# A planned attention kernel: the second half of each output sum gets another priority, and three figures of the planner change

## The chip, the cores and the metric

The kernel runs on one core of a Trainium2 chip. The metric is the device time of one execution in microseconds (us); lower is better. Before the change the median of 11 runs is 850.99 us (849.99 to 853.66).

## What is computed

One input `x` of 2048 tokens by 512 goes through two attention blocks with 32 heads of 16, and a gate mixes the two results.

```
x = A_x                                            # [1, 2048, 512] bf16
g = sigmoid((x * gate_w).sum(-1, keepdims=True))
# A: full attention, H=32, Dh=16
scores = einsum("bhqd,bhkd->bhqk", q, k) * Dh**-0.5
a = (softmax(scores) @ v, heads joined) @ A_wo
# B: each token looks at 8 earlier tokens, 2 apart (W, dil = 8, 2)
idx = pos[:, None] - (arange(8) * 2)[None, :]      # masked where idx < 0
b = (softmax(q . k[idx] * Dh**-0.5) @ v[idx], heads joined) @ B_wo
return g * a + (1 - g) * b
```

The gate's factors are folded into the normalisation of the two blocks, so that one output tile of 128 tokens is the sum of eight 128x128x512 matmuls: four with `A_wo`, four with `B_wo`.

## The kernel before

**Tiling.** The scores of block A are made in units: 128 keys by 512 queries of one head. Four heads form a group; 8 groups times 4 chunks of 512 queries make 32 periods (line 506) of 64 units each, 2048 units in all. A score matmul uses 32 rows of TensorE, so up to four heads run side by side. The product of probabilities and values ("PV") uses 17 columns per head, and again four heads side by side. Projections, output sums and transposes use the whole array. TensorE thus changes between three tiling modes: row tiles (scores), column tiles (PV), whole array (the rest).

**The exponential.** ScalarE takes most units. Two rings in PSUM take turns: ring A holds three units, ring B two (`act_stream`, line 972). TensorE fills a ring (`ring<-qt,kt_all`), ScalarE computes one `pT<-ring` over it (128x1536 or 128x1024), then the ring may be filled again. I call the fill of ring A a three-unit fill, that of B a two-unit fill, and the TensorE work that stands between one fill and the next a *slot*; it is named after the fill that opens it. The PV matmuls of five units usually stand together in the slot behind a two-unit fill.

**Units off ScalarE.** Some units are computed instead by VectorE (four passes, `ta<-w`, twice `ta<-ta,w`, `pd<-ta,w`, line 1093) or GpSimd (line 1128). Their scores go to one of two PSUM banks called `w` (line 450). A unit rides along with a fill (`rider`, line 1063) or goes alone (`solo`, line 1043). A *doubled* fill (line 1011) writes the same scores twice, which gives TensorE work at the end of a period, while its accumulator is closed; in other gaps `fill_pass` (line 847) adds matmuls with a zero weight (`acc<-ident,z`).

**Jobs.** Projections for both blocks, transposes and output sums need a `w` bank too. A 512-column job of four matmuls is the commonest. `final_job` (line 1301) makes one output tile: it yields its eight matmuls in two pieces of four (line 1322), the first (`w<-awo,oT`) with priority `30 + tt`, the second (`w<-bwo,obt`) with priority `GO`, 1.9; then VectorE copies the bank out (`osb<-w`, line 1380) and SyncE's queue stores it. Twelve tiles (the first three chunks) have four plus four matmuls; in the last chunk two tiles have seven in such pieces, and two are made by `direct_job` (line 1345) at the end.

**What sets the order.** The program is written out once, by a planner in Python (`class Plan`, line 52), which runs while the kernel is built. Every job is a generator that asks for an engine with a priority, a planned duration and a function that emits the instructions. `run` (line 222) keeps a planned clock for each engine and takes, for the engine that can go first, the ready request of the lowest priority number. The order in which it takes them is the order of the instructions on each engine; on the chip the engines follow it, and semaphores guard the data. What matters for the change:

- Fills have priority 0, PV from ScalarE's units a little over 1, `GO` pieces 1.9, jobs 2 and more.
- `fits` (line 216) lets a TensorE request of priority 2 or more start only if its planned end is not past `limit` (line 185), the planned time at which ScalarE runs out of queued work, less `refill`, 0.52; after 4 us of waiting it yields slowly. A request below 2 is never held by it.
- A TensorE piece of n passes is planned as `n * MM + SW`, with `MM` 0.2135 and `SW` 0.11 (lines 468, 469), the latter for the change of tiling mode; line 284 takes the same 0.11 off when it books how much the array streamed.
- `JW`, 0.8 (line 190), is how much planned VectorE work must be queued before a job that needs a `w` bank may start (`room_for_job`, line 200; it may anyway after 3 us), and above which a rider makes way for a waiting job (line 1074).

All instructions are emitted through one wrapper, so the profile gives all of them line 347; they are told apart by their tiles.

Of the kernel before, what the change touches and what calls it, by code (L numbers as in the profile page):

```python
# [51 lines left out]
class Plan:  # L52
# [13 lines left out]
    held = {"job": 0}  # L66
    streamed = deque()
    cap_job = 2
    refill = 0.52
    patience = 6.0  # L70

    def resource(self, name, n):
# [114 lines left out]

    passes = 0
    calm = False
    JW = 0.8  # L190
    JP = 3.0
    HUNG = 0.0
    ASL = 1.2
# [6 lines left out]
    def room_for_job(self, x, st):  # L200
        return not self.calm or st - x[7] > self.JP or self.dve_work(st) >= self.JW

# [19 lines left out]
    def run(self):  # L222
        while True:
            best = None
            for e, lst in self.ready.items():
                rs = []
                for x in lst:
                    g_ = self.gate(x[6])
                    if g_ is not None:
                        rs.append(max(x[2], g_))  # L230
                if rs:
                    st = max(self.free[e], min(rs))
                    if best is None or st < best[0]:
                        best = (st, 1, e)
            for r, lst in self.reqs.items():
                if lst and self.slots[r]:
                    st = max(min(x[0] for x in self.slots[r]), min(x[2] for x in lst))
                    if best is None or st <= best[0]:
                        best = (st, 0, r)
            if best is None:  # L240
                return
            st, kind, nm = best
            self.now = st
            if kind == 0:
                lst = self.reqs[nm]
                x = min(y for y in lst if y[2] <= st + 1e-9)
                lst.remove(x)
                s = min(y for y in self.slots[nm] if y[0] <= st + 1e-9)
                self.slots[nm].remove(s)
                self.advance(x[3], st, s[1])  # L250
            else:
                lst = self.ready[nm]
                ok = [y for y in lst if y[2] <= st + 1e-9 and self.gate(y[6]) is not None
                      and self.gate(y[6]) <= st + 1e-9]
                x = min(ok, key=lambda y: (y[0], y[1]))
                if nm == "pe" and 1 <= x[0] < 1.5 and st - x[2] < self.DEFER:
                    jobs = [y for y in lst if y[0] >= 2 and y[4] > 0.5 and y[7] <= st
                            and self.gate(y[6]) is not None and self.gate(y[6]) <= st + 1e-9]
                    y = min(jobs, key=lambda y: (y[0], y[1])) if jobs else None
                    if (y is not None and st + y[4] <= self.limit(st)  # L260
                            and (y[6] != "w" or self.room_for_job(y, st))):
                        x = y
                if nm == "pe" and self.feed_dve(st):
                    continue
                if nm == "pe" and x[6] == "w" and not self.room_for_job(x, st):
                    x[2] = max(x[2], st + 0.1)
                    continue
                if nm == "pe" and not self.fits(x, st):
                    for y in ok:
                        y[2] = max(y[2], st + 0.1)  # L270
                    continue
                lst.remove(x)
                if nm == "pe":
                    self.idle_fill(st, 1 + (x[6] is not None))
                if x[6] is not None:
                    slot = self.take(x[6], st)
                    self.held["job"] += x[6] == "w"
                    more = x[5](slot)
                else:
                    more = x[5]()  # L280
                if isinstance(more, float):
                    x[4] += more
                if nm == "pe":
                    self.stream(st, x[4] - 0.11 - self.thin)
                    self.thin = 0.0
                if CFG_DEBUG:
                    LOG.append((st, x[4], nm, getattr(x[3], '__name__', '?'), x[0]))
                self.free[nm] = st + x[4]
                self.advance(x[3], st + x[4] + self.LAT[nm], None)
# [3 lines left out]
def kernel(  # L293
# [62 lines left out]
    def mm(out_, lhsT, rhs, start, stop, **kw):  # L356
        return PE.matmul(out_, lhsT=lhsT, rhs=rhs, start=start, stop=stop, **kw)
# [108 lines left out]
    P.resource("py", 1)  # L466
    P.resource("pp", 2)
    MM = 0.2135
    SW = 0.11
    VP = 0.60  # L470
    GO = 1.9
    UR = 0.7
# [94 lines left out]
    def k_job(i, sc, rel, prio):  # L567
# [6 lines left out]
        def pe(s):  # L574
            w.open(s, [128, QW])
            for c in range(DC):
                mm(w.t[:], wkp[:, c, i].rearrange("p j d -> p (j d)"), xT[:, c, sc * QW:(sc + 1) * QW],
                   c == 0, c == DC - 1)
        yield ("pe", prio, 4 * MM + SW, pe, w.kind)
        k_left[0] -= 1  # L580
# [27 lines left out]
    def kpk_job(b, sc, rel, prio):  # L608
# [5 lines left out]
        def pe(s):  # L614
            w.open(s, [128, QW])
            for c in range(DC):
                mm(w.t[:], wkr[:, c, 128 * (b + 1):128 * (b + 2)], xT[:, c, sc * QW:(sc + 1) * QW],
                   c == 0, c == DC - 1)
        yield ("pe", prio, 4 * MM + SW, pe, "w")
        k_left[0] -= 1  # L620
# [48 lines left out]
    def qpk_job(c_, b, rel, prio):  # L669
# [6 lines left out]
        def pe(s):  # L676
            w.open(s, [128, QW])
            for c in range(DC):
                mm(w.t[:], wqr[:, c, 128 * (b + 1):128 * (b + 2)], xT[:, c, c_ * QW:(c_ + 1) * QW],
                   c == 0, c == DC - 1)  # L680
        yield ("pe", prio, 4 * MM + SW, pe, "w")

# [35 lines left out]
    def v_job(h0, h1, tb, TB, rel, prio):  # L718
# [7 lines left out]
        def pe(t0, t1):  # L726
            def f(s=None):
                if t0 == 0:
                    w.open(s, [128, TB, n])
                for tt in range(t0, t1):  # L730
                    for c in range(DC):
                        mm(w.t[:, tt, :], xT[:, c, (tb + tt) * 128:(tb + tt + 1) * 128],
                           wv[:, c, h0 * DH:h1 * DH], c == 0, c == DC - 1)
                P.thin = (t1 - t0) * (one - 4 * n / 2400.0)
            return f
        step = TB if TB < 8 else TB // 2
        one = 4 * max(0.0555, n / 2400.0)
        for t0 in range(0, TB, step):
            yield ("pe", GO if t0 else prio, one * step + SW, pe(t0, t0 + step)) + (("w",) if t0 == 0 else ())
        yield ("dve", prio, VP, lambda: V.tensor_copy(out=vp_all[:, tb:tb + TB, h0:h1, 0:DH],  # L740
# [9 lines left out]
    def q_job(p, rel, prio):  # L750
# [9 lines left out]
        def pe(s):  # L760
            w.open(s, [128, QW])
            for c in range(DC):
                mm(w.t[:], wqp[:, c, i].rearrange("p j d -> p (j d)"), xT[:, c, c_ * QW:(c_ + 1) * QW],
                   c == 0, c == DC - 1)
        yield ("pe", prio, 4 * MM + SW, pe, "w")
        st = {}

        def absq():
# [4 lines left out]
        yield ("wait", ev_sel[i])  # L773
        yield ("pe", GO, MM + SW, lambda: mm(w.t[:], selk_all[:, i, :], st["a"][:], False, True,
                                               skip_group_check=True))
# [287 lines left out]
    def rider(js, now=None):  # L1063
        now = P.now if now is None else now
        for p in (front[0], front[0] + 1):
# [7 lines left out]
            j = max(opts, key=lambda j_: len(pend[p][j_]))  # L1073
            if flying[0] and (not P.calm or P.dve_work(now) >= P.JW) and any(x[6] and x[0] < 4.0 + 0.3 * min(front[0] + UR, 16.3) for x in P.ready["pe"]):
                return None
# [225 lines left out]
    def final_job(c_, tt, last):  # L1301

        t = c_ * TPC + tt
        ncb = DC - 1 if last else DC
        for cb in range(ncb):
            yield ("wait", ev_ot.setdefault((c_, cb), Event()))
        yield ("wait", ev_obt[NT - 1 if last else t])
        prio = 30 + tt
        w = Bank()
        srcs = [(oT_tiles[c_][:, cb, tt * 128:(tt + 1) * 128], awo[:, cb, :]) for cb in range(ncb)]  # L1310
        srcs += [(obt_tiles[c_][:, cb, tt * 128:(tt + 1) * 128], bwo[:, cb, :]) for cb in range(DC)]

        def pe(a, b):
            def f(s=None):
                if a == 0:
                    w.open(s, [128, D])
                for z in range(a, b):
                    mm(w.t[:], srcs[z][0], srcs[z][1], z == 0, z == len(srcs) - 1)
            return f
        for a in range(0, len(srcs), 4):  # L1320
            b = min(len(srcs), a + 4)
            yield ("pe", GO if a else prio, (b - a) * MM + SW, pe(a, b)) + (("w",) if a == 0 else ())
        final_left[c_] -= 1
        if final_left[c_] == 0:
            yield ("set", ev_final[c_])
        if not last:
            yield from out_steps(t, w, None, prio)
            return

        def part():  # L1330
            if "t" not in fpart:
                fpart["t"] = work.tile([128, TPC, D], FP32, name="fpart", tag="ksh", bufs=2)
            V.tensor_copy(out=fpart["t"][:, tt, :], in_=w.t[:])
        yield ("dve", prio, VP, part)
        yield w.close()
        yield ("wait", ev_last[tt // 2])
        w = Bank("e")

        def tail(s):
            w.open(s, [128, D])  # L1340
            mm(w.t[:], oT_tiles[c_][:, DC - 1, tt * 128:(tt + 1) * 128], awo[:, DC - 1, :], True, True)
        yield ("pe", tt, MM + SW, tail, "e")
        yield from out_steps(t, w, fpart["t"][:, tt, :], tt)
# [353 lines left out]
```

## Time and profile before

| | |
|---|---|
| median of 11 runs | 850.99 us (849.99 to 853.66) |
| the profiled execution | 850.25 us, span 848.4 us |
| granted TensorE clock | 0.999 |
| ScalarE busy | 826.5 us, 97% of the span |
| VectorE busy | 765.8 us, 90% |
| TensorE busy | 756.2 us, 89% (matmuls in flight, not array at its peak) |
| GpSimd busy | 725.5 us, 86% |
| score activations | 717: 359 of 128x1536, 358 of 128x1024 |
| first and last of them start at | 17.84 us and 837.56 us |

The span is the time from the first to the last instruction; the execution has 1.85 us around it. An engine's busy time is the union of its instructions' times. Two neighbouring activations overlap in their records (a 128x1536 one lasts 1620 ns on average, a 128x1024 one 1197 ns, together 2.82 us, while a pair of them comes every 2.23 to 2.29 us), so a pause between them shows as idle time only after the overlap is used up. The distance from start to start is the better measure.

### The profile page before, as it was taken

How to read it: one execution, taken by the hardware profiler on the slowest of the kernel's cores; microseconds unless marked ns; L12 is line 12 of the kernel's file. 1: busy time of each engine (PE TensorE's matmuls, PEld its weight loads, DVE VectorE, ACT ScalarE, POOL GpSimd, SP SyncE). 2: the span in 40 equal slices, each digit the busy share in tenths (PEclk: the TensorE clock that was granted, in tenths of full speed). 3: DMA queues.
4: the chain of work that ended last, by engine and by line, in shares of the span. 5: the costliest groups of instructions: out<-in, count | busy, mean ns of one | idle time of the engine just before them, and what ended most of it. 6: DMA issues, size and time to landing. Idle time of an engine off the chain costs nothing.

```text
span 848.4 us, 15781 instructions
## 1 busy us (share of the span) xinstructions
PE 756.2 (89%) x5864; PEld 266.8 (31%) x5864; DVE 765.8 (90%) x1332; ACT 826.5 (97%) x748; POOL 725.5 (86%) x734
## 2 busy tenths in 40 slices
PE   9999999989998888888998988888898998888887
PEld 4432343333323332223333232333223233222222
DVE  5698889899999899998999899999989899999896
ACT  5999999999999999999999999999999999999996
POOL 2596886999799999899999999999899999997781
PEclk9999999999999999999999999999999999999999
DMA  9002304411444041303122413120313221201000
GB/s 295 6 14 88 100 27 140 153 64 39 129 118 163 27 130 31 112 19 100 39 89 71 129 34 130 58 81 8 106 32 112 87 83 24 63 13 58 14 1 26
DMA packets 72589, 63.84 MB, mean 75 GB/s; under 512 B 20528, under 2 KB 69168, under 8 KB 72512
## 3 DMA queue, kind: packets, MB, share of 16 engines
q1 hardware_dynamic: 71312, 62.57, 24.1%
q8 instruction: 46, 0.75, 0.4%
q10 hardware_dynamic: 1200, 0.26, 0.2%
q14 instruction: 31, 0.25, 0.1%
HBM read 46.14 MB, written 12.62 MB: 69 GB/s over the span
## 4 chain that ended last, share of the span: by engine, by line
ACT 66%; issue 20%; PE 11%; DMA 1%; DVE 1%; SPq 0%; ACTq 0%
ACT pT L347 65%; PE w L347 4%; PE ring L347 3%; PE acc L347 2%; ACT lg L347 1%; DMA xr<-in_A_x_dram 1%; DVE ta L347 0%; PE s L347 0%; SPq L347 0%; PE e L347 0%; DVE pd L347 0%; DVE qpk L347 0%; DVE osb L347 0%; DVE kvs L347 0%; ACT osc L347 0%
## 5 line engine op out<-in xcount | busy, mean ns | idle before, releaser
L347 ACT ACTIVATE pT<-ring 128x1536 bf16<-128x1536 f32 x717 | 816.5, 1409 | 6.7 <-PE ring L347 3.7
L347 PE MATMUL ring<-qt,kt_all 32*128 32x512 bf16 x1841 | 284.9, 380 | 82.6 <-ACT pT L347 70.2
L347 DVE SCALAR_TENSOR_TENSOR ta<-ta,w 128x512 f32<-128x512 f32 x476 | 317.3, 681 | 5.6
L347 POOL TENSOR_TENSOR prod<-prod 128x512 f32<-128x512 f32 (+1 forms) x208 | 240.4, 1166 | 5.5
L347 PE MATMUL acc<-pT,vp_all 128*17 128x512 bf16 x1793 | 221.4, 383 | 1.3 <-DVE accS L347 0.9
L347 PEld LDWEIGHTS <-kt_all 32*128 32x128 bf16 x2096 | 113.0, 91 | 335.8 <-issue 325.7
L347 PE MATMUL acc<-ident,z 128*17 128x512 bf16 (+5 forms) x773 | 197.3, 341 | 1.4 <-POOL ident masks.py:199 1.4
L347 DVE TENSOR_SCALAR ta<-w 128x512 f32<-128x512 uint16 x238 | 162.6, 686 | 36.4 <-PE w L347 34.3
L347 DVE SCALAR_TENSOR_TENSOR pd<-ta,w 128x512 uint16<-128x512 f32 x238 | 160.2, 678 | 2.5
L347 POOL TENSOR_TENSOR prod<-ksh,qb 128x512 f32<-128x512 bf16 x128 | 144.8, 1156 | 2.2
L347 POOL TENSOR_TENSOR prod<-vsh,lg 128x512 f32<-128x512 bf16 x128 | 136.7, 1098 | 2.8 <-DMA vsh<-kv_scr 0.3
L347 PE MATMUL w<-qt,kt_all 32*128 32x512 bf16 x255 | 95.5, 383 | 0.0
L347 PE MATMUL acc<-pd,vp_all 128*17 128x512 bf16 x255 | 83.1, 380 | 0.0
L347 PEld LDWEIGHTS <-z 128*17 128x17 bf16 (+1 forms) x780 | 54.0, 91 | 71.8 <-issue 43.2
L347 PEld LDWEIGHTS <-vp_all 128*17 128x17 bf16 x2048 | 40.5, 87 | 90.0 <-issue 89.8
L347 POOL TENSOR_TENSOR psc<-psc 128x512 f32<-128x512 f32 x51 | 60.9, 1193 | 3.9
L347 PE MATMUL w<-bw,xT 128*128 128x512 bf16 x192 | 49.7, 381 | 0.4
L347 POOL TENSOR_SCALAR psc<-psc 128x512 f32<-128x512 uint16 (+1 forms) x34 | 21.0, 618 | 31.8 <-DVE psc L347 29.6
L347 PEld LDWEIGHTS <-xT 128*128 128x128 bf16 x448 | 31.7, 97 | 28.9 <-issue 16.4
L347 POOL TENSOR_TENSOR lg<-lg,mx 128x256 f32<-128x256 f32 x16 | 10.1, 630 | 20.9 <-DVE mx L347 20.7
L347 DVE COPY accS<-acc 128x512 f32<-128x512 f32 (+1 forms) x33 | 21.9, 666 | 2.8 <-PE acc L347 2.7
L347 DVE CAST kvs<-w 128x512 bf16<-128x512 f32 x32 | 21.9, 684 | 0.9 <-PE w L347 0.7
(107 smaller groups left out, 453.1 us busy)
## 6 DMA issues: line engine op xcount, KB each, us to landing
ksh<-kv_scr SPq DMA_DIRECT2D x16, 1024.0 KB
vsh<-kv_scr SPq DMA_DIRECT2D x16, 1024.0 KB
kv_scr<-kvs SPq DMA_DIRECT2D x16, 256.0 KB
kt_all<-k_scr SPq DMA_DIRECT2D x6, 512.0 KB
q_scr<-qpk SPq DMA_DIRECT2D x24, 128.0 KB
qt<-q_scr SPq DMA_DIRECT2D x24, 128.0 KB
out_dram<-osb SPq DMA_DIRECT2D x14, 128.0 KB
xr<-in_A_x_dram SPq DMA_DIRECT2D x3, 512.0 KB
```

Source lines behind the costliest of these rows:

```text
L347: return chain_on(self._key, f(*a, **k))
```

## The change

Five figures change. The second piece of an output sum gets priority 2.0 in place of 1.9. The planned cost of a tiling change goes from 0.11 to 0.116, in both places. `refill` goes from 0.52 to 0.5, `JW` from 0.8 to 1.6. No instruction is written differently; the planner lays the program out anew, and the order on every engine differs from the early part of the kernel on.

```diff
-    refill = 0.52
+    refill = 0.5
...
-    JW = 0.8
+    JW = 1.6
...
                 if nm == "pe":
-                    self.stream(st, x[4] - 0.11 - self.thin)
+                    self.stream(st, x[4] - 0.116 - self.thin)
...
-    SW = 0.11
+    SW = 0.116
...
         for a in range(0, len(srcs), 4):
             b = min(len(srcs), a + 4)
-            yield ("pe", GO if a else prio, (b - a) * MM + SW, pe(a, b)) + (("w",) if a == 0 else ())
+            yield ("pe", 2.0 if a else prio, (b - a) * MM + SW, pe(a, b)) + (("w",) if a == 0 else ())
```

## The prediction

> **What bounds the kernel now.** First the page's busy times and the groups of instructions by form (tiles, shape and count; busy us, mean ns; idle before).
>
> ```profile
> PE 756.2 (89%) x5864; PEld 266.8 (31%) x5864; DVE 765.8 (90%) x1332; ACT 826.5 (97%) x748; POOL 725.5 (86%) x734
> ...
> L347 ACT ACTIVATE pT<-ring 128x1536 bf16<-128x1536 f32 x359 | 581.5, 1620 | 6.1 <-PE ring L347 3.7 <-PE w L347 1.1 <-PE acc L347 1.0
> L347 ACT ACTIVATE pT<-ring 128x1024 bf16<-128x1024 f32 x358 | 428.6, 1197 | 0.6 <-PE acc L347 0.6
> L347 PE MATMUL ring<-qt,kt_all 32*128 32x512 bf16 x1841 | 284.9, 380 | 82.6 <-ACT pT L347 70.2
> ```
>
> ScalarE never rests, and TensorE's fills wait for it (70.2 us, the longest single wait 0.5 us by the table of waits). So the time is the number of activations times their distance. From the starts of the 717 activations in the trace: undisturbed, the next one follows a 128x1536 after 1.330 us and a 128x1024 after 0.903 us, 2.233 us a pair. The span is then 17.84 (until the first) + 819.72 + 10.84 (from the last start to the end), and 819.72 = 358 pairs x 2.233 (799.4) + 16 other activations (`lg`) x 0.307 (4.9) + 15.4 us of lateness. That 15.4 is all that a better order can give back. 36 activations that come over 40 ns late hold 11.5 of it; the other 680 share 3.9, some 6 ns each.
>
> Next I read TensorE's and ScalarE's timelines around a late one (start us, us, what).
>
> ```profile
> 419.03 0.39 PE L347 MATMUL ring<-qt,kt_all 32*128 32x512 bf16 x3
> 419.04 0.39 PE L347 MATMUL w<-qt,kt_all 32*128 32x512 bf16 x1
> 419.36 1.04 PE L347 MATMUL w<-awo,oT 128*128 128x512 bf16 x4
> 420.33 0.39 PE L347 MATMUL ring<-qt,kt_all 32*128 32x512 bf16 x2
> 420.64 0.60 PE L347 MATMUL acc<-pT,vp_all 128*17 128x512 bf16 x5
> 421.18 1.04 PE L347 MATMUL w<-bwo,obt 128*128 128x512 bf16 x4
> 422.14 0.39 PE L347 MATMUL ring<-qt,kt_all 32*128 32x512 bf16 x3
> ```
>
> ```profile
> 417.44 4.71 ACT L347 ACTIVATE pT<-ring 128x1536 bf16<-128x1536 f32 x4
> 422.64 4.63 ACT L347 ACTIVATE pT<-ring 128x1536 bf16<-128x1536 f32 x4 [0.49 <-PE ring L347]
> ```
>
> The first half of an output sum stands behind a three-unit fill, the second behind the next two-unit fill and its five PV matmuls. From fill to fill this pair takes 422.14 - 419.03 = 3.11 us, 0.88 more than ScalarE's 2.233. The fill is late; ScalarE pauses 0.49 us, and by the starts loses 0.74, since overlap goes too. A pair with only one half would take 0.32 + 0.97 + 0.32 + 0.53 = 2.14 us and fit.
>
> Then I sorted all lateness by the slot in which TensorE stood. Second halves behind a two-unit fill, 8 of them (0.22 to 0.88): 4.93 us. Three other four-matmul jobs behind such fills (0.19, 0.07, 0.05): 0.31. Doubled fills that put one more pass before a three-unit fill's activation, 6 times (0.16 to 0.23): 1.18. A four-matmul job right behind a doubled fill, 8 times (0.02 to 0.71): 3.72. The rest, 1.4, is scattered. Against this, 84 four-matmul jobs behind a plain three-unit fill, without PV, cost 8 ns each (worst 0.20), no more than an empty slot.
>
> **The change, part by part.** It alters no instruction, only counts and order. I take both from the two built programs' instruction order and price each place with before's rows.
>
> *Second halves.* Of the 14 tiles with such a piece, before has 6 second halves behind a three-unit fill and 8 behind a two-unit one. After, 13 stand behind a three-unit fill, no PV beside them, and one behind a two-unit fill with three PV. The other jobs behind two-unit fills go from three to two. All such slots together: 11 at 5.24 us become three like the four in before whose fill had at most four PV (mean 0.215): 0.65. That is -4.6, and +0.15 for more jobs behind three-unit fills. Bounds: the row's worst (0.20) for each moved one would cost 8 x 0.2 = 1.6; its best nothing. I take 8 ns, the row that 84 slots give. No semaphore wait is added: the waiting is the planner's, and the order is fixed when the kernel is built. But the half sum holds one of two `w` banks one to two slots longer, so its copy (VectorE, 0.69) and its store on SyncE's queue come about 1 to 2 us later. In that queue the 187 transfers stay the same; the transposes and reads that the later store now follows mostly wait long for their data anyway (the last `obt` transpose starts at 788.2 us, its first use by the last chunk is at 806.0). I cost the store at nothing; a score read pushed back would cost at most the 1 to 2 us once.
>
> *The price of banks held longer, and of `JW`.* Units off ScalarE fall from 255 to 250 (VectorE 238 to 234, GpSimd 17 to 16). ScalarE gets one pair more, 360 + 359 activations: +2.23 us, certain, on the path. VectorE loses 4 x 4 passes + 1 copy, 17 x 0.68 = 11.6 us, GpSimd 6 instructions, about 5.4 us; neither sets the end, so that gives nothing.
>
> *Doubled fills.* Before has 15 doubled two-unit fills and 6 doubled three-unit ones, after 12 and 12. Twelve lateness places in place of six, at 0.18 to 0.20: +1.16. Of these, jobs right behind fall from 8 to 2 (priced 0.54 and 0.33): -2.84. Six new slots, a doubled three-unit fill with five PV behind, occur nowhere in before; doubled two-unit fills with PV behind cost 0.01 to 0.03 each (once 0.16). I take 0.1 for all, bounds 0 and 0.9.
>
> *Single places.* A value-projection job behind two-unit fill and five PV is new; nearest are the second halves there: +0.62 (0.19 to 0.88). Transposes behind two-unit fill and five PV go from four to eight, mean 0.08: +0.3. A query job's last matmul behind seven PV (0.22) goes away. Two more odd slots +0.2, small shifts of the common ones -0.3. Together +0.6.
>
> *The planned tiling change.* The trace has 0.31 to 0.32 from the last score matmul to the first of another mode, against 0.215 within a mode: a change costs 0.10, and the planner now believes 0.116. The Trainium skill, "TensorEngine Tiling (Array Packing)", Key Properties, says that changing the mode drains TensorE, and this speaks against the change: a second half moved from behind PV into a slot of its own adds a drain. By that rule 8 moved halves add 8 x 0.10 = 0.8 us of TensorE. By the rows that is hidden, since a 2.14 us pair still waits for ScalarE; and over the whole program the changes number 1416 before and 1415 after, as filler went elsewhere. I take 0.
>
> *Filler.* Larger planned work leaves smaller planned gaps: zero-weight filler in the accumulator falls from 745 matmuls with 301,696 columns to 702 with 264,896; at 0.215 us per 512 that is 15.5 us less TensorE work. "TensorE: Matmul & The Clock Gate", Part 1, says that an idle window of about 3.4 us puts the clock back to half. By the trace no wait of a fill exceeds 0.5 us and the granted clock is 0.999 of full; pairs without any filler are common before too. By the rows 0; by the rule, see the last rival.
>
> Sum: -4.6 + 0.15 + 2.23 + 1.16 - 2.84 + 0.1 + 0.6 = -3.2 us. The profiled execution, 850.25 (span 848.4), would become 847.05; it lies 0.74 below the median of 850.99. The median forecast is 850.99 - 3.2 = 847.8. Start and tail stay: the order up to the first activations is the same, and behind the last one the same pieces follow.
>
> **Rivals.** What the measurement can tell from no change is about 0.2%, 1.7 us: faster is below 849.3, slower above 852.7.
>
> *The forecast* (0.52): 847.8; its own range 846.5 to 849.0.
>
> *The order cleans up more* (0.17). The 1.4 us of scattered lateness goes as well, as the planner's dearer mode change leaves reserve. -3.2 - 1.4 = -4.6: 846.4. For it: slot pairs whose passes and changes add up to over 2.4 us fall from 28 to 9. Against: three of the scattered ones (0.05 to 0.08) stand in slots that fit.
>
> *The plan drifts* (0.25). What comes of doubled fills (-1.7) is luck of the layout, and the chip pays it elsewhere, because riders or banks are not free when the plan says so. Then -1.5: 849.5, range 848.7 to 850.8. For it: only the 8 second halves are aimed at; a new order moves every other job. Against: the count of jobs behind doubled fills is in the order itself. That second halves are not moved at all is excluded by the order.
>
> *The clock falls* (0.06). With 15.5 us less filler, a window near a period's end is too idle and the clock halves for about 3.4 us. A pair with a job then takes 8 passes of 0.43 and four changes, 3.8 us, 1.6 late. Two such windows with one job each just eat up the gain of 3.2; from three on the kernel is slower, and four windows give +3.2: 854.2. Against: the clock stayed full in all 40 slices of before.
>
> **How the numbers follow.** Likeliest 847.8. The range 845.6 to 850.4 leaves out the clock case, the upper end of the drift and the lower end of the clean order; the open bounds (1.6, 0.9 and 0.3 upward, 0.7 and 1.4 downward, not all together) lie in it. Faster by over 0.2%: 0.52 + 0.17 + a quarter of the drift = 0.75; same 0.19; slower 0.06.
>
> **What would show it.** 719 activations; pairs still 2.233 us apart where undisturbed; lateness near 10 us in place of 15.4; behind `w<-bwo,obt` no late fill save perhaps one near 692 us; lateness before the doubled three-unit fills near 12 x 0.2; the clock at 0.999; 10.8 us after the last activation. I am wrong if pauses of ScalarE appear at other jobs, or fills wait for VectorE to free a `w` bank.

## The result and the profile after

The kernel after takes 848.28 us in the median of 12 runs (846.78 to 850.46); before is 851.1 us over the 47 runs shown beside it. The ratio is 0.9965, 95% interval 0.9955 to 0.9974: 2.8 us faster, where 3.2 was forecast. The profiled execution took 847.90 us with a span of 846.1 us, 2.3 us less than before's span.

The page's busy times of the kernel after, then three of its groups by form:

```profile
PE 748.4 (88%) x5828; PEld 266.4 (31%) x5828; DVE 754.9 (89%) x1315; ACT 827.5 (98%) x750; POOL 719.8 (85%) x728
```

```profile
L347 ACT ACTIVATE pT<-ring 128x1536 bf16<-128x1536 f32 x360 | 585.5, 1626 | 2.7 <-PE ring L347 2.5
L347 ACT ACTIVATE pT<-ring 128x1024 bf16<-128x1024 f32 x359 | 431.9, 1203 | 0.4 <-PE acc L347 0.3
L347 PE MATMUL ring<-qt,kt_all 32*128 32x512 bf16 x1858 | 286.8, 381 | 88.6 <-ACT pT L347 70.7
```

ScalarE has one pair of activations more and is still the bound; VectorE is 11 us less busy, but does not set the end. TensorE's timeline at one of the moved sums (start us, us, what), and ScalarE's over the same stretch:

```profile
423.12 0.39 PE L347 MATMUL ring<-qt,kt_all 32*128 32x512 bf16 x3
423.45 1.04 PE L347 MATMUL w<-awo,oT 128*128 128x512 bf16 x4
424.42 0.39 PE L347 MATMUL ring<-qt,kt_all 32*128 32x512 bf16 x2
424.74 0.39 PE L347 MATMUL acc<-pT,vp_all 128*17 128x512 bf16 x3
424.75 0.39 PE L347 MATMUL acc<-pd,vp_all 128*17 128x512 bf16 x1
424.96 0.38 PE L347 MATMUL acc<-pT,vp_all 128*17 128x512 bf16 x2
425.38 0.39 PE L347 MATMUL ring<-qt,kt_all 32*128 32x512 bf16 x3
425.40 0.39 PE L347 MATMUL w<-qt,kt_all 32*128 32x512 bf16 x1
425.71 1.04 PE L347 MATMUL w<-bwo,obt 128*128 128x512 bf16 x4
```

```profile
419.15 13.88 ACT L347 ACTIVATE pT<-ring 128x1536 bf16<-128x1536 f32 x12
```

First and second half stand behind successive three-unit fills, 425.38 - 423.12 = 2.26 us apart where before's pair took 3.11, and ScalarE runs twelve activations without a pause.

The span splits as before's did, by the starts of the 719 activations: 18.54 until the first, 817.27, and 10.27 from the last start. 817.27 = 801.65 (359 pairs of 2.233) + 4.9 (`lg`) + 10.7 of lateness. The lateness by slot, us, with activations over 40 ns late counted by place:

| slot | before | forecast | after |
|---|---|---|---|
| four-matmul jobs behind a two-unit fill, second halves among them | 5.24 | 0.65 | 0.50 |
| such jobs behind a three-unit fill | 0.48 | 0.63 | 1.04 |
| before a doubled three-unit fill | 1.18 | 2.34 | 2.48 |
| jobs right behind a doubled fill | 3.7 | 0.88 | 0.61 |
| other places | 0.92 | 1.6 | 2.34 |
| all below 40 ns | 3.88 | 3.9 | 3.74 |
| sum | 15.4 | 10.0 | 10.7 |

Not all of this is a fill that comes late. At the jobs right behind a doubled fill ScalarE mostly waits for something else, in the kernel before as well. TensorE's timeline at one of them, then ScalarE's:

```profile
98.68 0.39 PE L347 MATMUL ring<-qt,kt_all 32*128 32x512 bf16 x3
99.00 0.39 PE L347 MATMUL acc<-pT,vp_all 128*17 128x512 bf16 x3
99.01 0.38 PE L347 MATMUL acc<-pd,vp_all 128*17 128x512 bf16 x1
99.23 0.38 PE L347 MATMUL acc<-pT,vp_all 128*17 128x512 bf16 x1
```

```profile
99.70 1.45 ACT L347 ACTIVATE pT<-ring 128x1536 bf16<-128x1536 f32 x1 [0.33 <-PE acc L347]
```

The activation starts 1.02 us after its fill began, where 0.50 is usual: it waits for PV (`acc`), which still reads the `pT` tile that it is to write, and which the job in front of the fill has put off. Six of before's eight such places, 3.5 of their 3.7 us, are of this kind; the eight second halves (4.9 us) are late fills. After the change three places are of it: 0.49 us right behind a doubled fill, and 0.44 and 0.27 at jobs behind three-unit fills.

One of the "other places" alone costs 0.70 us, and no job stands in its slot. Around it, each engine's busy time by stretch (us, then PE, PEld, DVE, ACT, POOL with instructions, granted clock, DMA):

```profile
590.00:597.00 7.00, 5.62 (x46) 1.87 (x45) 4.71 (x9) 7.00 (x8) 6.69 (x8) 1.00 0.54 158
597.00:601.00 4.00, 4.00 (x24) 0.91 (x23) 4.00 (x8) 3.68 (x4) 2.30 (x3) 0.57 0.16 55
601.00:608.00 7.00, 5.57 (x53) 1.85 (x47) 6.56 (x13) 7.00 (x8) 6.52 (x8) 1.00 0.00 0
```

In the middle row the granted clock is 0.57: for 3.41 us the trace records half clock. TensorE is then busy throughout, and ScalarE has 3.68 of 4 us. The runs differ in how often this happens, before as well as after, so their mean granted clock and their time go together. Before, over the 65 runs that were taken beside the experiments: six at 1.000 take 850.0 us in the median, seven at 0.993 or less 853.4. After: one at 1.000 takes 846.78, two at 0.990 take 850.4. A straight line through each set falls by 314 us (before) and 349 us (after) per 1.0 of clock, which is 0.6 to 0.7 us on average for each 3.41 us window at half clock (0.002 of the mean). At a clock of 1.000 the lines stand at 850.4 and 847.0, the second uncertain by about 0.2. I use such lines below to compare kernels at equal clock.

### The profile page after: what moved, and what is told of

Read it like the earlier page. It is cut to its first block, busy times and chain, and to the rows that moved or that the text cites. A ratio compares the mean times of both kernels' runs of the same rounds, so it can differ in the third digit from the quotient of the medians.

```text
span 846.1 us, 15697 instructions
## 1 busy us (share of the span) xinstructions
PE 748.4 (88%) x5828; PEld 266.4 (31%) x5828; DVE 754.9 (89%) x1315; ACT 827.5 (98%) x750; POOL 719.8 (85%) x728
## 4 chain that ended last, share of the span: by engine, by line
ACT 73%; issue 21%; PE 6%; POOL 0%; ACTq 0%; POOLq 0%
ACT pT L347 72%; PE acc L347 2%; PE ring L347 1%; PE w L347 1%; ACT lg L347 1%; PE s L347 1%; PE e L347 0%; ACT osc L347 0%; ACT e L347 0%; POOL ident masks.py:199 0%; POOL identf masks.py:197 0%; POOL ident masks.py:197 0%; ACTq L347 0%; POOLq L1681 0%
## 5 line engine op out<-in xcount | busy, mean ns | idle before, releaser
L347 DVE SCALAR_TENSOR_TENSOR ta<-ta,w 128x512 f32<-128x512 f32 x468 | 312.9, 682 | 5.7
L347 PEld LDWEIGHTS <-kt_all 32*128 32x128 bf16 x2108 | 115.1, 91 | 337.8 <-issue 321.9
L347 DVE TENSOR_SCALAR ta<-w 128x512 f32<-128x512 uint16 x234 | 160.1, 686 | 41.2 <-PE w L347 39.6
L347 PE MATMUL acc<-ident,z 128*17 128x512 bf16 (+4 forms) x730 | 180.5, 333 | 1.4 <-POOL ident masks.py:199 1.4
L347 DVE SCALAR_TENSOR_TENSOR pd<-ta,w 128x512 uint16<-128x512 f32 x234 | 158.3, 679 | 2.9
L347 PEld LDWEIGHTS <-z 128*17 128x17 bf16 (+1 forms) x732 | 50.4, 92 | 69.0 <-issue 44.0
L347 POOL TENSOR_TENSOR psc<-psc 128x512 f32<-128x512 f32 x48 | 57.3, 1193 | 3.6
```

Source lines behind the costliest of these rows:

```text
L347: return chain_on(self._key, f(*a, **k))
```

## The experiments

My theory is the slot theory: ScalarE is late when the TensorE work from one fill of a ring to the next does not fit into ScalarE's 2.233 us a pair, so lateness can be counted from the order. The rivals are drift (the plan runs apart from the chip, and lateness comes up elsewhere) and the clock.

**Which edit does it.** Three kernels take edits of the change singly or leave one out.

```diff
# e1_prio_only: the priority alone
-            yield ("pe", GO if a else prio, ...
+            yield ("pe", 2.0 if a else prio, ...
# e2_all_but_prio: after with
-            yield ("pe", 2.0 if a else prio, ...
+            yield ("pe", GO if a else prio, ...
# e3_prio_sw: after with
-    refill = 0.5
+    refill = 0.52
-    JW = 1.6
+    JW = 0.8
```

> Only the priority of the second piece goes to 2.0; the three planner figures stay as before. By the built order one second half is left behind a two-unit fill (8 before), but jobs right behind a doubled fill stay at 8 (2 after the whole change) and there are 719 activations. Slot theory (lateness belongs to the slot, priced by the rows of before): +2.2 for the extra pair, -3.4 of lateness, so -1.2 us: 849.9. If the priority alone carried the whole gain: 848.3, as with the whole change. Drift theory (what the slots show is luck of the layout): anywhere within 1 us of before, with lateness not tied to the counted slots.

Measured: 848.69 us, ratio 0.9967 (0.9955 to 0.9979), against the whole change's 0.9965. The lateness is as expected, 11.7 us in the trace for 12.0: one second half behind a two-unit fill is late, by 0.06 us (before: 8, 4.9 us), and jobs behind doubled fills still cost 3.4 us (before 3.7). From the first to the last activation this gives 1.4 us. The expectation had no term for the end: from the last activation on this order takes 9.44 us, before's 10.8. The start is 0.8 later, so that the two profiled executions, both near full clock, differ by 2.1. At equal clock the gain is 1.9 us by the runs at 1.000 (four at 848.1 in the median, before's six at 850.0) and 2.6 by the lines (847.9 and 850.4). So the priority is worth more than the forecast 1.2 us, and its order has another tail as well as less lateness.

> The three planner figures as after, the second piece at 1.9 as before. By the built order 8 second halves stand behind a two-unit fill, 5 jobs behind doubled fills, 718 activations. Slot theory: +1.3 for one activation, -0.9 of lateness: 851.5, no gain. If the planner figures carry the gain (mode change priced right): near 848.3.

Measured: 853.55 us, ratio 1.0026 (1.0017 to 1.0036). In the medians the other three figures without the priority make the kernel slower. Its trace has 7 late second halves with 5.5 us; three windows at half clock add to it, with single activations 1.6 and 0.8 us late there, and 12 runs have a mean clock of 0.992 against 0.997 of before. At equal clock its line stands at 850.9, uncertain by 0.4, against before's 850.4: no gain and no clear loss, as the slot theory expected. The rest of the loss goes with the clock.

> Priority 2.0 and the planned tiling change of 0.116; refill and JW as before. By the built order: 719 activations, one second half behind a two-unit fill, 3 jobs behind doubled fills (9 doubled three-unit fills). Slot theory: +2.2 and -6.1: -3.9 us, 847.2, a little better than the whole change. If JW or refill carry part of the gain: above 848.3.

Measured: 848.07 us, ratio 0.9959 (0.9948 to 0.9971), not distinguishable from the whole change or from the priority alone (three runs at a clock of 1.000 take 847.9 to 848.1). The expected 847.2 is missed by 0.9, with 10.8 us of lateness in its trace for the expected 9.3. So the gain hangs on the priority; what `SW`, `JW` and `refill` add to it is below what the medians resolve. At equal clock this kernel and e1 stand at 848.0 and 847.9, the whole change at 847.0. That hints at 0.9 us from `JW` and `refill`, but no run changes these two alone.

**Taking the second halves away.** To price them where they stand, the planner still books them, so that everything else keeps its place, but emits nothing. The part of `B_wo` is left out of 14 tiles.

```diff
# in final_job, e4_before_no_second_half and e5_after_no_second_half
-                for z in range(a, b):
-                    mm(w.t[:], srcs[z][0], srcs[z][1], z == 0, z == len(srcs) - 1)
+                for z in range(a, b if a == 0 else a):
+                    mm(w.t[:], srcs[z][0], srcs[z][1], z == 0, z == 3)
```

> The kernel before, with the order of all other instructions kept: the planner books the second piece of every output sum but no matmul is emitted for it, so the part of B_wo is left out of 14 of the 16 output tiles. 54 matmuls fewer, 717 activations. Slot theory: the lateness of 4.9 us behind the 8 second halves in two-unit slots goes, nothing else: 851.1 - 4.9 = 846.2. Drift theory (the plan runs ahead of the chip and the lateness shows up at whatever comes next): the lateness moves on to other jobs, 849 to 851.

Measured: 848.93 us, ratio 0.9962 (0.9949 to 0.9976): by the medians 2.7 us off, not 4.9. Two of its five runs have a clock of 1.000 and take 847.8 and 848.2, 2.0 us below before's 850.0 at that clock. The 4.9 us at the eight places are gone from the trace, but not all of it is saved. TensorE's timeline in this kernel, two slots after the first place:

```profile
423.05 0.39 PE L347 MATMUL acc<-pT,vp_all 128*17 128x512 bf16 x3
423.84 0.38 PE L347 MATMUL acc<-pd,vp_all 128*17 128x512 bf16 x1 [0.41 <-DVE pd L347]
423.85 0.39 PE L347 MATMUL acc<-pT,vp_all 128*17 128x512 bf16 x2
424.16 0.39 PE L347 MATMUL ring<-qt,kt_all 32*128 32x512 bf16 x2
424.17 0.39 PE L347 MATMUL w<-qt,kt_all 32*128 32x512 bf16 x1
424.49 1.04 PE L347 MATMUL w<-awo,oT 128*128 128x512 bf16 x3
```

TensorE now comes early and waits 0.41 us for VectorE's `pd`; then the next job stands behind a two-unit fill, and 0.39 us of lateness appears there. Such jobs rise from 0.31 to 1.72 us in all. So drift is right in part: an order that was laid out with late fills hides other waits behind them. Two windows at half clock in the profiled execution cost it another 2.8 us. This leaves 3.5 of the 4.9 us in the trace, and the runs at full clock show 2.0; where the other 1.5 goes stays open. Here, then, taking a stall out of an order that stays as it is gained about half of it.

> The kernel after, with its order kept, and the second piece of 14 output sums left out (the part of B_wo is missing in those tiles; 54 matmuls fewer). Slot theory: the pieces now stand where TensorE has room, only 0.27 us of lateness lies on them, so nothing is gained: 848.0 (fast windows of the clock apart). If moving them only hid their cost elsewhere: 1.5 us or more below the kernel after, under 846.8. Clock theory: 11.7 us less TensorE work means a few more windows at half clock, 0.7 us each: up to 849.

Measured: 850.68 us over 13 runs, ratio 0.9992 (0.9983 to 1.0001). With work taken away the median is 2.4 us above after's. Its clock is 0.986 to 0.998, mean 0.9915 (after: 0.9959). The one run at 0.998 takes 847.4, and six of after at 0.998 take 847.3 to 849.0; lateness in the two traces is 10.77 and 10.71 us. At equal clock its line stands at 847.3, after's at 847.0, each uncertain by 0.2 to 0.4: the second halves cost nothing after the change, as the slot theory says. What the median loses goes with the clock, which is lower without their work. This is not so in every order: e4 leaves out the same work and has a mean clock of 0.996, like before's 0.9965 in the runs beside it.

**The clock.** Filler first taken away, then lengthened; then the doubled fills taken away.

```diff
# e6_after_no_filler: fill_pass books the time and emits nothing once an accumulator is open
-            mm(acc_tiles[p][32 * j:32 * j + DH + 1, 0:m], z32[:, 0:DH + 1], filling(m), False, False, ...
-                mm(wt[0:32, 0:m], z32[:], filling(m), True, True, tile_position=(0, 0))
# e8_after_more_filler (e11_before_more_filler: the same on before)
-        while done < n:
-            m = min(QW, n - done)
+        while done < n + 128:
+            m = min(QW, n + 128 - done)
# e7_after_no_doubled_fills
-    TWICE = 0.60
+    TWICE = 0.0
```

> The kernel after, with the zero-weight filler in the accumulator planned but not emitted (702 matmuls, 264,896 columns, 110 us of array time; the result is the same). In the runs so far windows of 3.41 us at half clock follow windows in which the array streams under about half of the time. Clock theory: without filler the usual pair streams 4 passes of 0.213 in 2.233 us, 0.38, so nearly all windows are at half clock; a pair with a four-matmul job then takes 3.8 us: 131 such pairs lose 1.6 us each, about 200 us: 1000 to 1080, granted clock near 0.55. If filler is not needed for the clock: 848 or a little less.

Measured: 897.62 us, ratio 1.0557 (1.0534 to 1.0579), clock 0.79. The clock row of its page, in tenths by slice, and ScalarE's wait for fills:

```profile
PEclk9988899899895669757899777675659996575586
```

```profile
ACT pT L347 <- PE ring L347: 32.7, 49, 2.2
```

The direction is the clock theory's, the size a third of its lowest figure: the mean clock is 0.79 and not 0.55, and of the 719 activations only 141 are over 40 ns late. Some 24 of these stand at four-matmul jobs behind three-unit fills, most of them 1.0 us late where 1.6 was expected.

> The kernel after with no doubled fill (threshold 0; 24 fills lose their second pass). Slot theory: the 2.5 us of lateness before doubled three-unit fills and 0.6 right behind doubled fills go: 848.3 - 3.1 = 845.2. Clock theory: the ends of periods now stream too little, and of some 24 period ends up to half are followed by a window at half clock, 0.7 us each: +4 to +8, 849 to 853, clock under 0.99.

Measured: 850.62 us, ratio 1.0002 (0.9992 to 1.0011), clock 0.982 to 0.992. The kernel is as slow as before again, and the clock has its part in this. By stretch, with the columns of above:

```profile
736.00:743.00 7.00, 5.20 (x44) 1.69 (x43) 6.93 (x13) 7.00 (x7) 6.92 (x7) 1.00 0.09 21
743.00:750.00 7.00, 6.88 (x45) 2.06 (x43) 5.10 (x12) 5.90 (x6) 6.92 (x7) 0.51 0.09 19
750.00:757.00 7.00, 5.79 (x49) 2.02 (x48) 6.97 (x13) 7.00 (x7) 6.77 (x7) 1.00 0.09 19
```

For two windows the clock is at half, and ScalarE loses 1.1 of 7 us. The trace has four windows, with 3.9 us of lateness at them, against 0.7 in the trace of after. The slot theory's 3.1 us are not gained beside this, though. The planner books the second pass too, so without it the order of the jobs is laid out anew from 270 us on, which the expectation did not see. Outside the windows the lateness is 9.2 us, after's 10.0: the doubled fills' 3.1 us are gone, and 2.3 of new lateness stand at other places (0.49 at an output sum at 433 us). So this run shows that the kernel without doubled fills has the lower clock; it does not price the doubled fills in a fixed order.

> The kernel after, with each piece of filler 128 columns longer than the planner books (310,336 columns in place of 264,896, 18.9 us more of TensorE work, in gaps where fills now wait 0.3 to 0.4 us for ScalarE). Clock theory: granted clock 1.0 in nearly every run, 0.053 us of a gap used: 846.8 to 847.2, the best runs of the kernel after, and a narrower scatter. If the scatter has another cause: 848.3 and the same scatter; if the gaps are too short: later fills, 849 and more.

Measured: 847.91 us, ratio 0.9963 (0.9952 to 0.9975); five runs at clocks of 0.994 to 0.998. 18.9 us more TensorE work cost no lateness (10.80 us), but the clock theory's expectation fails: no run has a clock of 1.000, the mean is 0.997 (after: 0.996), and a window near 600 us is at half clock in the profiled execution. No gain beyond the interval.

> The kernel before with each filler piece 128 columns longer than booked, order kept. Clock theory: its slower runs (851 to 853.5, clock 0.999 to 0.992) go and the fastest stay: 850.0 to 850.9. If the longer filler costs lateness in before's tighter gaps: 851.5 and more.

Measured: 851.57 us, ratio 1.0001 (0.9993 to 1.0009), with clocks from 0.995 to 1.000 and a mean of 0.9975, before's 0.9972. The clock theory's expectation fails again. Which windows fall in before's slower runs no trace shows, since those that were kept are at full clock. In the trace of this execution, at full clock, the lateness is 15.40 us and the eight second halves hold 4.88 of it, exactly as in the first trace of before.

**More of the same.** Since a held-back second half helps output sums, every second piece gets 2.0, with and without the longer filler.

```diff
# e9_all_second_pieces_2; e10_all_2_more_filler: also the longer filler
-    GO = 1.9
+    GO = 2.0
```

> The kernel after with priority 2.0 for every second piece (query jobs and value projections too). By the built order 717 activations (719 after), one second half of an output sum behind a two-unit fill, 4 jobs behind doubled fills, 9 doubled three-unit fills. Slot theory with the rows of before: -2.2 for the pair saved, -0.3 of lateness: 848.3 - 2.5 = 845.8. Clock theory: two units more on VectorE and GpSimd change nothing, but windows at half clock come by chance; 845.8 to 848.

> As the run before, and each filler piece 128 columns longer than booked. Slot theory: as the run before, 845.8. Clock theory: fewer windows at half clock than without the longer filler, 845.5 and under 2 us of scatter.

Measured: 856.32 us, ratio 1.0048 (1.0033 to 1.0063), and 855.65 us, ratio 1.0055 (1.0038 to 1.0073). One of the first kernel's six executions took 1189 us, for a reason that stays open; its trace is of that one and the ratio leaves it out, so I read the second kernel's trace. Both expectations fail by 10 us, at two places that the count of slots does not see. The first activation starts at 21.84 us in place of 18.54, because the query of the first period is itself such a job and its second piece (`w<-absq,selk_all`) was held: it starts at 19.46 us, in after at 16.87. And after 102 us one activation is 4.3 us late. The chain that ended last, there, in order of time:

```profile
100.53 0.60 DVE vp_all L347
101.13 0.60 DVE ta L347
101.73 0.02 issue
101.76 0.69 DVE pd L347
102.45 0.60 DVE vp_all L347
103.05 2.47 DVE ta L347 x4
105.52 0.61 DVE accS L347
106.13 0.04 issue
106.17 0.82 PE acc L347 x9
```

VectorE is behind: four passes of units go ahead of the copy `accS`, and TensorE waits for this copy before it starts the next accumulator:

```profile
106.17 0.60 PE L347 MATMUL acc<-pT,vp_all 128*17 128x512 bf16 x6 [1.46 <-DVE accS L347]
```

## Why the prediction was right, point by point

*ScalarE's distance bounds the kernel.* Right: the undisturbed distances after are 1.330 and 0.903 us, and one pair more costs 2.23.

*Second halves, -4.6 with the jobs beside them, +0.15 behind three-unit fills.* Measured by the table -4.7 and +0.6. The one left behind a two-unit fill was not late at all (1 ns). The +0.6 is four times the forecast, and 0.71 of that row are two places where ScalarE waits for PV and not for the fill: a projection at 204 us (0.44), and a second half in the last chunk, behind a three-unit fill and a slot with five PV (0.27), which no row of before had at that place. That the priority carries this is shown by e1 (ratio 0.9967 alone, one late second half of 0.06 us) and e2 (1.0026 without it, seven with 5.5).

*Doubled fills, +1.16 - 2.84 + 0.1.* Measured +1.3 and -3.1; the slots with five PV behind a doubled three-unit fill cost 0.02 each, like any. The size of the -2.84 was right, but it was read as a fill that comes late, and most of it is ScalarE's wait for PV. The forecast's doubt, that this is luck which the chip takes back, did not come true in the trace. In time it is little: e1, which lacks it, stands at 847.9 at equal clock, the whole change at 847.0, of which each is uncertain by 0.2.

*Single places, +0.6.* Measured +1.4, 0.7 of it the window at half clock at 597 us. The new value-projection place cost 0.28, not 0.62.

*Filler, 0.* This step stood on too little: "by the rows 0" was read from one execution of before that happened to have a clean clock. Whether it was wrong stays open. Over the runs the mean clock falls from 0.9972 to 0.9959, which at 314 to 349 us per 1.0 would be 0.4 to 0.5 us, but with 12 runs of after the fall itself is uncertain by 0.001, and e3, with less filler in its trace than after (706 matmuls for 730), has 0.9976 over five runs. At equal clock the gain is 850.4 - 847.0, 3.5 us before rounding, where 3.2 was forecast; 2.8 is what is left in the medians. The last rival treated half-clock windows as an accident that the change might bring, while both kernels have them in most runs. Its 1.6 us is the price where a job stands in the window (1.3 and 1.4 at the two of e4, 1.64 at one of e2); the average is 0.6 to 0.7.

*Start and tail, 0.* In the two profiled executions the start is 0.7 us later and the tail 0.55 shorter. The start is scatter: with the same early order the first activation comes between 17.75 and 18.62 us in the traces of after, e1, e3, e5, e7 and e8. The tail is not: 10.25 to 10.32 us in the traces of after, of e5 and e8, which have its order, and of e7; 10.68 to 10.82 in the three of before's order (before, e4, e11). The slot behind the last three-unit fill has one `acc<-pd` less after the change; whether that is the cause wasn't tried. "The same pieces follow" was thus not quite true.

*The sum.* That it comes so near is in part luck. Between the first and the last activation the two traces differ by 2.45 us, 0.8 less than forecast, nearly all of it the window at half clock; the shorter tail, which had no term, gives 0.55 of this back, and the start takes 0.7 again.

## What to carry to other kernels

Where one engine is fed by another in a fixed rhythm, add up the feeder's work from hand-over to hand-over, and sort the late ones by what stood between: here 8 places of 717 held a third of all lateness, and counting the new order against those rows gave 3.2 us where the runs gave 2.8. Such a count sees only the feeder: it missed the start and VectorE's backlog in e9 and e10, and taking work out of a laid-out order (e4) gave back about half of the stall. Ask at each late place whether the fed engine waited for its input or for room for its output; the count gives the same size, but the cure differs. Look at the granted clock of several runs, not of one profile, before costing filler at nothing, and compare kernels at equal clock.

## What the runs showed of the hardware

TensorE's clock falls to half for windows of 3.41 us (or several in a row) on a single core whose TensorE never waits longer than 0.6 us for a fill in the trace of after, 0.9 in that of e2. With 0.213 us per 512 columns, the array streams 0.63 of the time in the median window of after. The 3.41 us before ten such windows or rows of windows, in the traces of after, e2, e4, e5, e7 and e8, streamed 0.49; 0.44 and 0.30; 0.53 and 0.48; 0.42; 0.46, 0.47 and 0.44; 0.51. So about half idle can be enough, but this share does not decide: in the same traces some twenty windows that streamed 0.42 to 0.48 were followed by full clock.

The busy time of TensorE's row (matmuls in flight, as the profile gives it) separates better. In the same order it was 0.73; 0.62 and 0.47; 0.70 and 0.70; 0.64; 0.67, 0.65 and 0.62; 0.75, with one more in e10 at 0.74. Of the 1624 other windows at full clock in these seven traces, 53 were busy for 0.75 or less, and one for less than 0.67. Between 0.67 and 0.75 it stays open what decides.

The Trainium skill, "TensorE: Matmul & The Clock Gate", Part 1, gives one idle window of about 3.4 us as what puts the clock back; here no window was idle throughout. The same part tells of another kernel whose clock swings because TensorE idles briefly and often between groups of matmuls, and these traces are nearer to that. Leaving out 11.6 us of needed matmuls (e5) lowered the mean clock from 0.9959 to 0.9915 in one order; in another (e4) it did not.
